# Two-bank PSUM tiles taken as two one-bank tiles in a fused RWKV-7 and gated feed-forward kernel

## The chip, the core and the metric

The kernel runs on one core of one Trainium2 chip. Five engines work side by side, each through its own queue in order: TensorE (PE in the profile; its weight loads are PEld), VectorE (DVE), ScalarE (ACT), GpSimd (POOL) and the DMA-issuing SyncE (SP). TensorE writes its results into PSUM, which this kernel uses as eight banks of 512 float32 per partition; VectorE and ScalarE read them from there. The metric is the device time of one execution in microseconds.

## The reference

Two blocks are computed one after the other, in float32 on the chip. The first is a recurrence over 768 time steps, for 4 batches of 8 heads with 40 features; the second is a feed-forward layer with `h * cos(h)` between two matrices.

```python
# attention block, per batch b and head h; state is 40 x 40
for t in range(S):
    y[:, :, t] = einsum('bhd,bhde->bhe', r_t, state)
    Sa = einsum('bhde,bhe->bhd', state, a_t)
    state = state * w_t[:, :, None, :] - einsum('bhd,bhe->bhde', Sa, b_t) \
          + einsum('bhd,bhe->bhde', v_t, k_t)
# feed-forward block on x = y as (3072 tokens, 320)
h = x @ w_in            # 320 x 2048
out = (h * cos(h)) @ w_out   # 2048 x 320
```

## The kernel before

The recurrence is done in 24 units, u = 0 to 23. A unit is 64 time steps of two batches with all their heads. Inside a unit the steps are dense matrices, and only the state passes from unit to unit of the same two batches. The work of a unit is cut into segments, each a short helper function that gives TensorE 4 to 64 small matmuls into a PSUM tile and then lets ScalarE or VectorE read that tile:

- `p1_w`, `p1_a`, `p1_b`, `p1_n` (for two units at a time): transposes of w, a and b (tiles wT, aps, bT), then the products of b and a within the unit (tile nps). ScalarE copies nps to `nt` (line 484), from which VectorE computes a triangular inverse in many small steps (lines 530 and 534); ScalarE later copies another part of nps (line 503).
- `p2_v`, `p2_k`, `p2_g`: transposes of v, r and k (tiles vT and kT), then the tile gram, which VectorE masks into `ag` (line 688) and `vvm` (line 692).
- `ch_t`, `ch_q`: the state is transposed (tile sT, ScalarE's copy `s` in line 708) and multiplied by r (tile qps); ScalarE copies the result into `qz` (line 721).
- `ch_ag`, `ch_xa`: the tile x0ps is filled in two parts and read by both engines, bank 0 by ScalarE (line 752) and bank 1 by VectorE (line 753).
- `ch_s`: the tile sps, the inverse times x0. ScalarE copies the state columns of both banks into `sm` (line 770, two instructions), VectorE masks the rest of both banks into `sm` (line 775, two instructions).
- `ch_z`: the tile dps. Its first half needs only kn and vvm, its second half `sm`. VectorE reads it in lines 801 and 812.

Beside this run the pieces of the feed-forward block: `first_a` and `first_b` fill two one-bank tiles ph in the pool `ps_h`. ScalarE rounds them (line 899), VectorE subtracts (line 903), ScalarE takes absolute value and sine (lines 906 and 907), VectorE multiplies into `gT` (line 910). `second` multiplies `gT` with w_out into the tile po of the pool `ps_o`, which ScalarE scales into `ot` (line 931).

All tiles of the recurrence's segments come from the pool `ps_a` through `at(name)`: a tile of two banks, and two such tiles, so four banks in all. Segments that need one bank (kT, sT, below, beside, xps) take a two-bank tile through `one(None, name)` and leave its second bank unused. A tile is given out again when all readers of its predecessor are done. A framework sets the semaphores, tile by tile: an instruction that touches a PSUM tile waits for the last one on another engine that touched the same tile, also where both only read and where their banks differ.

The order on every engine is written out by hand: `PLAN`, a list of some 1,900 words, each a segment (`xa9`, `s9`), a piece of the feed-forward block (`M`), one of the six later steps of a piece (`r`), a step of the inverse (`i`), a step of decoding the feed-forward weights (`c`) or a load (`Lk9`). `^` adds one dummy matmul on the identity ahead of the next tile (`busy`). The engines follow this order exactly; no scheduler moves anything. Loading of a weight piece (`seg_f`, SP's queue) is started from within `w_item` when a leading piece is done.

Of the kernel before, what the change touches and what calls it, by code (L numbers as in the profile page):

```python
# [20 lines left out]
def kernel(  # L21
# [38 lines left out]
    ps_a = ctx.enter_context(tc.tile_pool(name="ps_a", bufs=2, space=bass.MemoryType.PSUM))  # L60
# [311 lines left out]
    def p1_w(u):  # L372
        ps = at("wT")
        for i in range(2):
            turned(ps[:, i], nat["w", u + i])
        for i in range(2):
            if u < 4:
                nc.scalar.copy(G["w1"][:, i, :, 0:1], b4(ps[:, i])[:, :, 0:1])
                nc.vector.memset(ps[:, i, ::C], 0.0)
            wb = ring.tile([P, 4 * P + 1], F32, tag="wb", name="wb")  # L380
            if u < 4:
                nc.vector.tensor_tensor_scan(
                    wb[:, 1:], ps[:, i], flat(G["w1"][:, i]), 0.0, ALU.mult, ALU.add
                )
            else:
                nc.scalar.copy(wb[:, 1:], ps[:, i])
# [23 lines left out]
    def p1_a(u):  # L410
        if u >= 4:
            ps = at("aps")
            for i in range(2):
                turned(ps[:, i], nat["a", u + i])
            for i in range(2):
                a_W(u + i, ps[:, i])
# [13 lines left out]
    def p1_b(u):  # L430
        ps = at("bT")
        for i in range(2):
            turned(ps[:, i], bn_b[(u + i) % 7])
        for i in range(2):
            bT = sb3.tile([P, 4, P], F32, tag="opT", name="bT")
            nc.scalar.copy(bT.rearrange("p j t -> p (j t)"), ps[:, i])
            G["bT", u + i] = bT

    def p1_n(u):
        if u == 2:  # L440
            ps = [one(ps_h, "nps") for _ in range(2)]
        else:
            pair = at("nps")
            ps = [pair[:, e] for e in range(2)]
# [35 lines left out]
        else:  # L480

            for n in range(4):
                o = 8 * Q * (n % 2)
                nc.scalar.copy(
                    G["nt"][quad[n], :, u % 4 : u % 4 + 2],
                    pair[quad[n], :, o : o + 8 * Q].rearrange("p e (c j t) -> p t c e j", c=2, j=HH),
                )
# [171 lines left out]
    def p2_v(u):  # L659
        ps = at("vT")  # L660
        turned(ps[:, 0], nat["v", u])
        turned(ps[:, 1], nat["r", u])
        G["vT", u] = sb3.tile([P, 4, P], F32, tag="opT", name="vT")
        G["rT", u] = sb2.tile([P, 4, P], F32, tag="rT", name="rT")
        nc.scalar.copy(G["vT", u].rearrange("p j t -> p (j t)"), ps[:, 0])
        nc.scalar.activation(
            G["rT", u].rearrange("p j t -> p (j t)"), ps[:, 1], ACTF.Copy, scale=0.5 / math.pi
        )

    def p2_k(u):  # L670
        ps = at("kT")
        turned(ps[:, 0], kn_b[u % 2])
        G["kT", u] = sb3.tile([P, 4, P], F32, tag="opT", name="kT")
        nc.scalar.copy(G["kT", u].rearrange("p j t -> p (j t)"), ps[:, 0])

    def p2_g(u):
        kT, vT, aT, rT = G["kT", u], G["vT", u], G["aT", u], G["rT", u]
        ps = at("gram")
        for x, y, o in ((kT, aT, 0), (vT, rT, HH)):
            for j in range(4):  # L680
                for bb in range(NB):
                    for e in range(2):
                        mm(
                            ps[blk[bb], e, (o + j) * C : (o + j + 1) * C], x[half[e], j, blk[bb]],
# [3 lines left out]
        nc.vector.tensor_tensor(  # L688
            ag.rearrange("p (e j) t -> p e (j t)", e=2), ps[:, :, : HH * C],
            su.rearrange("p j t -> p (j t)").unsqueeze(1).to_broadcast([P, 2, HH * C]), ALU.mult,  # L690
        )
        nc.vector.tensor_tensor(
            pick(vvm[u % 2], 0, (HH * NW + D, 2), (NW, HH), (1, C)),
            ps[:, :, HH * C :].rearrange("p e (j t) -> p e j t", t=C),
            su.unsqueeze(1).to_broadcast([P, 2, HH, C]), ALU.mult,
        )
# [3 lines left out]
    def ch_t(u):  # L700
        ps = at("sT")
        z = qz[u % 2]
        G["s", u] = sb1.tile([P, 2 * NB, P], F32, tag="s", name="s")
        for i in range(2 * NB):
            nc.tensor.transpose(  # L705
                ps[:, 0, i * P : (i + 1) * P], z[:, i // 2, i % 2, C : C + P], ident
            )
        nc.scalar.copy(G["s", u].rearrange("p i e -> p (i e)"), ps[:, 0])

    def ch_q(u):  # L710
        ps = at("qps")
        z = qz[u % 2]
        for i in range(2 * NB):
            for e in range(2):
                for f in range(2):
                    mm(
                        ps[half[e], f, i * C : (i + 1) * C], G["s", u][half[f], i, half[e]],
                        G["rT", u][half[f], 2 * (i % 2) + e, blk[i // 2]], i == 0,
                    )
        for rows in half:  # L720
            nc.scalar.copy(  # L721
                pick(z[rows], 0, (NZ - C, 2), (NZ, 2 * NB), (1, C)),
# [554 lines left out]
```

## Time and profile before

| what | value |
|---|---|
| runs | 783.51, 782.81 and 779.36 us, median 782.81 us |
| profiled execution, its own time | 778.82 us |
| span of the profiled execution, first to last instruction | 776.9 us |
| TensorE busy | 752.7 us |
| VectorE busy | 504.9 us |
| ScalarE busy | 416.5 us |
| GpSimd busy | 184.0 us |
| mean granted TensorE clock | 0.994 |

A row of instruction groups reads: line, engine, operation, what is written and from what, shape, count, then busy time in us and the mean of one in ns, then the idle time of the engine just before these instructions and what ended it. A row of the waits reads: the waiting engine with tile and line, the releaser, then total us, times, longest us. A row of the timeline reads: start and duration in us, engine, line, operation, tiles, count, and in brackets the idle time before it with its releaser; neighbouring instructions of a kind are merged, so that the duration is that of the group. The ends of matmuls are modelled, so what counts for TensorE is when its next group starts.

### The profile page before, as it was taken

The page shows a single profiled execution, that of the slowest core. Times are in us where ns is not written, and L with a number is a line of the kernel's source. Part 1 is how long each engine was busy: PE and PEld are TensorE (multiplying, and loading weights), DVE is VectorE, ACT ScalarE, POOL GpSimd, SP SyncE. Part 2 cuts the span into 40 slices and gives each one's busy share as a digit, 9 for nine tenths or more (in the row PEclk, how much of TensorE's full clock was granted, in tenths as well). Part 3 has the DMA queues.
Part 4 walks back from the last instruction along what each step waited for, and adds up shares of the span by engine and source line. Part 5 has one row for each costly group of instructions (what it writes and reads, how often), then busy time and mean ns, then how long its engine had stood idle before and what let it go on. Part 6 is the DMA issues. An engine that isn't in the chain of part 4 may idle for free.

```text
span 776.9 us, 27804 instructions
## 1 busy us (share of the span) xinstructions
PE 752.7 (97%) x12118; PEld 593.5 (76%) x12118; DVE 504.9 (65%) x965; ACT 416.5 (54%) x762; POOL 184.0 (24%) x320
## 2 busy tenths in 40 slices
PE   8999999899999999999999999999999999999995
PEld 6877877677777877777878778787877787777773
DVE  6796889899769965578835677844476743334221
ACT  1354677655484566546475655465644464544432
POOL 5224635411331242120222202340101121201000
PEclk9999999999999999999999999999999999999998
DMA  9553675362334424423411421423022110200100
GB/s 141 113 128 76 151 183 141 94 140 42 59 103 79 88 61 77 112 72 61 83 34 38 96 62 21 87 54 71 3 46 55 34 23 19 56 10 16 33 17 18
DMA packets 180913, 54.36 MB, mean 70 GB/s; under 512 B 156344, under 2 KB 176440, under 8 KB 180792
## 3 DMA queue, kind: packets, MB, share of 16 engines
q1 hardware_dynamic: 173368, 51.43, 30.2%
q10 hardware_dynamic: 7424, 1.15, 1.0%
q8 instruction: 96, 1.57, 0.8%
q14 instruction: 25, 0.20, 0.1%
HBM read 41.68 MB, written 10.81 MB: 68 GB/s over the span
## 4 chain that ended last, share of the span: by engine, by line
PE 78%; DVE 10%; ACT 5%; issue 2%; DMA 2%; SPq 1%; POOL 1%; ACTq 0%; DVEq 0%; POOLq 0%
PE ph L75 24%; PE po L75 23%; PE dps L75 5%; PE x0ps L75 4%; PE beside L75 3%; PE gram L75 3%; PE sps L75 3%; DVE inv L534 2%; PE vT L364 2%; DVE inv_tmp L530 2%; PE nps L75 1%; PE below L75 1%; DMA words<-in_moe_w_in_dram 1%; PE bT L364 1%; PE qps L75 1%
## 5 line engine op out<-in xcount | busy, mean ns | idle before, releaser
L75 PE MATMUL po<-w_out_sb,gT 128*128 128x320 f32 x768 | 220.5, 438 | 0.0
L75 PEld LDWEIGHTS po<-w_out_sb,gT 128*128 128x128 f32 x768 | 141.3, 190 | 56.5 <-issue 2.4
L75 PE MATMUL ph<-xT,w_in_sb 128*128 128x256 f32 x768 | 183.2, 386 | 0.7 <-DVE gT L910 0.7
L75 PEld LDWEIGHTS ph<-xT,w_in_sb 128*128 128x128 f32 x768 | 140.6, 190 | 30.1 <-issue 9.4
L899 ACT ACTIVATE turns<-ph,rnd 128x512 f32<-128x512 f32 x96 | 62.9, 685 | 130.8 <-PE ph L75 129.7
L903 DVE SCALAR_TENSOR_TENSOR turns<-turns,ph 128x512 f32<-128x512 f32 x96 | 63.3, 679 | 79.7 <-ACT turns L899 79.6
L910 DVE TENSOR_TENSOR gT<-ph,turns 128x512 f32<-128x512 f32 x96 | 65.0, 684 | 33.4 <-ACT turns L907 33.1
L802 POOL TENSOR_TENSOR qz<-qz,wc 128x160 f32<-128x160 f32 x44 | 21.0, 480 | 221.2 <-DVE qz L801 220.3
L907 ACT ACTIVATE turns<-turns,half_pi 128x512 f32<-128x512 f32 x96 | 69.3, 722 | 3.1
L906 ACT ACTIVATE turns<-turns 128x512 f32<-128x512 f32 x96 | 60.2, 627 | 14.4 <-DVE turns L903 13.8
L534 DVE TENSOR_TENSOR inv<-inv,inv_tmp 128x31 f32<-128x31 f32 (+15 forms) x155 | 59.5, 384 | 5.3
L530 DVE TENSOR_TENSOR inv_tmp<-u,inv 128x31 f32<-128x31 f32 (+15 forms) x155 | 56.9, 367 | 3.1
L75 PE MATMUL ph<-xT,w_in_tail 64*64 64x256 f32 (+1 forms) x696 | 51.8, 383 | 0.0
L399 DVE RECIPROCAL rw<-nat_w 128x320 f32<-128x320 f32 x20 | 42.8, 2142 | 0.3 <-POOL kn L653 0.3
L817 POOL TENSOR_TENSOR yt<-yt,wb 128x512 f32<-128x512 f32 x24 | 31.2, 1302 | 42.5 <-DVE yt L812 42.4
L753 DVE COPY x<-x0ps 128x416 f32<-128x416 f32 x24 | 14.2, 591 | 38.6 <-ACT x L752 38.4
L721 ACT COPY qz<-qps 40x512 f32<-40x512 f32 x44 | 25.4, 577 | 22.4 <-PE qps L75 22.0
L75 PEld LDWEIGHTS ph<-xT,w_in_tail 64*64 64x64 f32 (+1 forms) x696 | 26.8, 138 | 13.6 <-issue 8.3
L400 POOL TENSOR_TENSOR bn<-nat_b,rw 128x320 f32<-128x320 f32 x22 | 19.3, 878 | 73.3 <-DVE rw L399 71.5
L775 DVE TENSOR_TENSOR sm<-sps,su 128x256 f32<-128x256 f32 x48 | 18.0, 417 | 25.1 <-ACT sm L770 21.4
L688 DVE TENSOR_TENSOR ag<-gram,su 128x512 f32<-128x512 f32 x24 | 16.5, 686 | 21.4 <-PE gram L75 21.3
L653 POOL TENSOR_TENSOR kn<-nat_k,rw 128x320 f32<-128x320 f32 x24 | 22.0, 915 | 31.7 <-PE sT L705 11.2
(181 smaller groups left out, 1178.0 us busy)
## 6 DMA issues: line engine op xcount, KB each, us to landing
rp<-in_r_dram SPq DMA_DIRECT2D x96, 40.0 KB
out_dram<-ot SPq DMA_DIRECT2D x24, 160.0 KB
vp<-in_v_dram SPq DMA_DIRECT2D x92, 40.0 KB
xd<-yt SPq DMA_DIRECT2D x44, 80.0 KB
nat_a<-in_a_dram SPq DMA_DIRECT2D x43, 80.0 KB
nat_k<-in_k_dram SPq DMA_DIRECT2D x42, 80.0 KB
nat_b<-in_b_dram SPq DMA_DIRECT2D x41, 80.0 KB
ws<-in_w_dram SPq DMA_DIRECT2D x5, 640.0 KB
```

Of the source, the lines that this page charges most:

```text
L75: nc.tensor.matmul(o, lhsT=lhsT, rhs=rhs, start=start, stop=stop, skip_group_check=True)
L364: nc.tensor.transpose(ps[:, i * P : (i + 1) * P], x[:, 2 * i : 2 * i + 2].rearrange("p e d -> p (e d)"), ident)
L399: nc.vector.reciprocal(rw, wn)
L530: nc.vector.tensor_tensor(tmp, u[:, j : j + 1, :j].to_broadcast([P, Q - j, j]), x[:, j:, j : j + 1].to_broadcast([P, Q - j, j]), ALU.mult,)
L534: nc.vector.tensor_tensor(x[:, j:, :j], x[:, j:, :j], tmp, ALU.subtract)
L721: nc.scalar.copy(pick(z[rows], 0, (NZ - C, 2), (NZ, 2 * NB), (1, C)), ps[rows, :, : 2 * NB * C].rearrange("p f (i t) -> p f i t", t=C),)
L817: nc.gpsimd.tensor_tensor(yt.rearrange("p j b t -> p (j b) t"), yt.rearrange("p j b t -> p (j b) t"), wx, ALU.mult)
L899: nc.scalar.activation(n, u, ACTF.Identity, bias=rnd, scale=1.0)
L903: nc.vector.scalar_tensor_tensor(ns[e], ns[e], -ROUND, us[e], ALU.add, ALU.subtract)
L906: nc.scalar.activation(n, n, ACTF.Abs)
L907: nc.scalar.activation(n, n, ACTF.Sin, bias=half_pi, scale=-2.0 * math.pi)
L910: nc.vector.tensor_tensor(gT[:, 2 * e : 2 * e + 2].rearrange("p f t -> p (f t)"), us[e], ns[e], ALU.mult)
```

## The change

`ps_a` gives four tiles of one bank each instead of two tiles of two banks. `at(name)` returns a list of two such tiles, and `one(None, name)` takes a single one, so that kT, sT, below, beside and xps occupy one bank. Every `ps[:, i]` becomes `ps[i]`. Readers that took both banks in one instruction are cut by bank:

- gram: two VectorE instructions of 512 elements per partition become four of 256 (`ag` for bank 0 and 1, then `vvm` for bank 0 and 1).
- qps: two ScalarE copies, each of 40 partitions and both banks, become two copies of all 128 partitions and one bank. For this TensorE computes 64 instead of 40 output partitions per matmul, with as many matmuls as before.
- nps, for units from 4 on: four ScalarE copies (one for each 32 partitions, both banks) become six, three for each bank: first all 128 partitions, then 32 partitions twice, which replace what the first wrote there.
- sps: the order becomes ScalarE bank 0, VectorE bank 1, ScalarE bank 1, VectorE bank 0. In each bank the second reader waits for the first.

The loads of weight pieces stand in `PLAN` as words of their own (`f7` and so on) at the places where they were started before. In the built program the order on GpSimd's and SyncE's queues is the same as before; on TensorE, ScalarE and VectorE it differs only in the instructions named here.

```diff
-    ps_a = ctx.enter_context(tc.tile_pool(name="ps_a", bufs=2, space=bass.MemoryType.PSUM))
+    ps_a = ctx.enter_context(tc.tile_pool(name="ps_a", bufs=4, space=bass.MemoryType.PSUM))
...
-    def at(name):
-        ps = ps_a.tile([P, 2, 512], F32, tag="at", name=name)
-        busy(ps[:, 0])
-        return ps
+    def at(name, n=2):
+        tiles = []
+        for _ in range(n):
+            tiles.append(ps_a.tile([P, 512], F32, tag="at", name=name))
+            busy(tiles[-1])
+        return tiles
 
     def one(pool, name):
         if pool is None:
-            return at(name)[:, 0]
+            return at(name, 1)[0]
...
     def p1_n(u):
-            for n in range(4):
-                o = 8 * Q * (n % 2)
-                nc.scalar.copy(
-                    G["nt"][quad[n], :, u % 4 : u % 4 + 2],
-                    pair[quad[n], :, o : o + 8 * Q].rearrange("p e (c j t) -> p t c e j", c=2, j=HH),
-                )
+            for e in range(2):
+                for n in (0, 1, 3):
+                    rows, o = quad[n] if n else every, 8 * Q if n else 0
+                    nc.scalar.copy(
+                        G["nt"][rows, :, u % 4 : u % 4 + 2, e, :],
+                        ps[e][rows, o : o + 8 * Q].rearrange("p (c j t) -> p t c j", c=2, j=HH),
+                    )
...
     def p2_g(u):
-        nc.vector.tensor_tensor(
-            ag.rearrange("p (e j) t -> p e (j t)", e=2), ps[:, :, : HH * C],
-            su.rearrange("p j t -> p (j t)").unsqueeze(1).to_broadcast([P, 2, HH * C]), ALU.mult,
-        )
+        for e in range(2):
+            nc.vector.tensor_tensor(
+                ag[:, HH * e : HH * (e + 1)], b4(ps[e])[:, :HH], su, ALU.mult
+            )
...
     def ch_q(u):
-                        ps[half[e], f, i * C : (i + 1) * C], G["s", u][half[f], i, half[e]],
+                        ps[f][full[e], i * C : (i + 1) * C], G["s", u][half[f], i, full[e]],
...
-        for rows in half:
+        for f in range(2):
             nc.scalar.copy(
-                pick(z[rows], 0, (NZ - C, 2), (NZ, 2 * NB), (1, C)),
-                ps[rows, :, : 2 * NB * C].rearrange("p f (i t) -> p f i t", t=C),
+                pick(z, f * (NZ - C), (NZ, 2 * NB), (1, C)), b4(ps[f][:, : 2 * NB * C]),
             )
...
     def ch_xa(u):
-        nc.scalar.copy(x0[0], ps[:, 0, : 4 * NW])
-        nc.vector.tensor_copy(x0[1], ps[:, 1, : 4 * NW])
+        nc.scalar.copy(x0[0], ps[0][:, : 4 * NW])
+        nc.vector.tensor_copy(x0[1], ps[1][:, : 4 * NW])
...
     def ch_s(u):
-        for e in range(2):
+        def state(e):
             nc.scalar.copy(
                 pick(sm[e], C, (2 * NW - C, 2), (NW, 2), (1, D)),
-                pick(ps[:, e], C, (2 * NW - C, 2), (NW, 2), (1, D)),
+                pick(ps[e], C, (2 * NW - C, 2), (NW, 2), (1, D)),
             )
-        for e in range(2):
+
+        def masked(e):
             nc.vector.tensor_tensor(
                 pick(sm[e], 0, (2 * NW + D, 2), (NW, 2), (1, C)),
-                pick(ps[:, e], 0, (2 * NW + D, 2), (NW, 2), (1, C)),
+                pick(ps[e], 0, (2 * NW + D, 2), (NW, 2), (1, C)),
                 su.rearrange("p (f m) t -> p f m t", f=2), ALU.mult,
             )
+
+        state(0)
+        masked(1)
+        state(1)
+        masked(0)
```

More of the change, by code (lines that the diff above doesn't have):

```diff
@@ L442, in p1_n @@
         else:
-            pair = at("nps")
-            ps = [pair[:, e] for e in range(2)]
+            ps = at("nps")
         for i in range(2):
@@ L660, in p2_v @@
         ps = at("vT")
-        turned(ps[:, 0], nat["v", u])
-        turned(ps[:, 1], nat["r", u])
+        turned(ps[0], nat["v", u])
+        turned(ps[1], nat["r", u])
         G["vT", u] = sb3.tile([P, 4, P], F32, tag="opT", name="vT")
         G["rT", u] = sb2.tile([P, 4, P], F32, tag="rT", name="rT")
-        nc.scalar.copy(G["vT", u].rearrange("p j t -> p (j t)"), ps[:, 0])
+        nc.scalar.copy(G["vT", u].rearrange("p j t -> p (j t)"), ps[0])
         nc.scalar.activation(
-            G["rT", u].rearrange("p j t -> p (j t)"), ps[:, 1], ACTF.Copy, scale=0.5 / math.pi
+            G["rT", u].rearrange("p j t -> p (j t)"), ps[1], ACTF.Copy, scale=0.5 / math.pi
         )
     def p2_k(u):
-        ps = at("kT")
-        turned(ps[:, 0], kn_b[u % 2])
+        ps = one(None, "kT")
+        turned(ps, kn_b[u % 2])
         G["kT", u] = sb3.tile([P, 4, P], F32, tag="opT", name="kT")
-        nc.scalar.copy(G["kT", u].rearrange("p j t -> p (j t)"), ps[:, 0])
+        nc.scalar.copy(G["kT", u].rearrange("p j t -> p (j t)"), ps)
     def p2_g(u):
@@ L687, in p2_g @@
         ag = sb1.tile([P, H, C], F32, tag="ag", name="ag")
-        nc.vector.tensor_tensor(
-            ag.rearrange("p (e j) t -> p e (j t)", e=2), ps[:, :, : HH * C],
-            su.rearrange("p j t -> p (j t)").unsqueeze(1).to_broadcast([P, 2, HH * C]), ALU.mult,
-        )
[L692 to L696, printed above, removed]
+        for e in range(2):
+            nc.vector.tensor_tensor(
+                ag[:, HH * e : HH * (e + 1)], b4(ps[e])[:, :HH], su, ALU.mult
+            )
+        for e in range(2):
+            nc.vector.tensor_tensor(
+                pick(vvm[u % 2], e * (HH * NW + D), (NW, HH), (1, C)),
+                b4(ps[e])[:, HH:], su, ALU.mult,
+            )
         G["ag", u] = ag
     def ch_t(u):
-        ps = at("sT")
+        ps = one(None, "sT")
         z = qz[u % 2]
@@ L789, in ch_z @@
                         mm(
-                            ps[(half if s else full)[e], bb, j * NW : (j + 1) * NW],
+                            ps[bb][(half if s else full)[e], j * NW : (j + 1) * NW],
                             n[blk[bb], 2 * j + e, : D if s else DP],
@@ L830, in straight @@
             G["xT", u // 2] = sb2.tile([P, 3, 2 * P], F32, tag="xT", name="xT")
-        ps = at("xps")[:, 0]
+        ps = one(None, "xps")
         for i, j in ((0, 0), (0, 1), (1, 1), (1, 2), (1, 3)):
@@ L1126, in w_item @@
                 w_count[0] += 1
-                if m in follower:
-                    seg_f(follower[m])
+                done.add(name)
+        leader = {n: m for m, n in follower.items()}
         def seg_f(m):
+            if m in leader:
+                needs(f"p{leader[m]}")
             if m == 13:
```

112 lines of the change are left out of this document (56 added, 56 removed).

## The prediction

> **What bounds the kernel now.** I began with the page's list of engines and its chain of work that ended last.
>
> ```profile
> PE 752.7 (97%) x12118; PEld 593.5 (76%) x12118; DVE 504.9 (65%) x965; ACT 416.5 (54%) x762; POOL 184.0 (24%) x320
> ...
> PE 78%; DVE 10%; ACT 5%; issue 2%; DMA 2%; SPq 1%; POOL 1%; ACTq 0%; DVEq 0%; POOLq 0%
> ```
>
> TensorE is the bound, and the change takes no matmul from it. What can be won is TensorE's idle time alone. The busy time by stretches shows where that lies; the columns are the stretch, its length, then busy us and instructions of each engine.
>
> ```profile
> 0.00:150.00 150.00, 139.42 (x2593) 112.46 (x2594) 122.71 (x221) 76.76 (x146) 63.99 (x115) 0.99 0.58 129
> 150.00:460.00 310.00, 305.05 (x5156) 241.65 (x5155) 227.26 (x453) 181.11 (x336) 75.22 (x133) 1.00 0.36 78
> 460.00:704.00 244.00, 243.72 (x4028) 191.94 (x4026) 134.73 (x261) 130.73 (x235) 42.25 (x70) 1.00 0.18 38
> 704.00:777.00 73.00, 64.53 (x356) 47.47 (x344) 20.18 (x33) 27.85 (x46) 2.55 (x2) 0.96 0.07 22
> ```
>
> Idle are 10.6, 4.9, 0.3 and 8.5 us. The last is the tail after the last matmuls, which the change doesn't touch. So at most some 16 us are to be had, all before 460 us; after that point TensorE can only lose. The table of waits says which of these 16 us have to do with two readers in one tile, or with a tile that wasn't free yet.
>
> ```profile
> DVE x L753 <- ACT x L752: 38.4, 19, 7.8
> DVE sm L775 <- ACT sm L770: 21.4, 8, 6.3
> PE dps L75 <- DVE ws L176: 2.2, 1, 2.2
> PE sps L75 <- DVE x L753: 1.1, 3, 0.7
> PE dps L75 <- DVE sm L775: 0.9, 2, 0.7
> PE ph L75 <- DVE gT L910: 0.7, 2, 0.5
> PE sT L705 <- ACT rt L647: 0.4, 1, 0.4
> PE gram L75 <- DVE x L753: 0.2, 1, 0.2
> ```
>
> VectorE stands 59.8 us behind ScalarE in line for a bank that ScalarE doesn't read. That looks like much, but TensorE's own waits in these rows are only 5.5 us: most of VectorE's waiting is covered by feed-forward matmuls.
>
> **The change, part by part.** *x0ps.* In the built program VectorE's copy now waits for TensorE and no longer for ScalarE. Around 140 us, where TensorE waits longest, the rows are:
>
> ```profile
> 139.32 0.51 ACT L752 COPY x<-x0ps 128x416 f32<-128x416 f32 x1
> ...
> 137.12 0.69 DVE L281 SCALAR_TENSOR_TENSOR w_in_sb<-w_in_sb,w_out_sb 128x512 f32<-128x512 f32 x1
> 139.86 0.59 DVE L753 COPY x<-x0ps 128x416 f32<-128x416 f32 x1 [2.05 <-ACT x L752]
> 144.11 0.76 DVE L775 TENSOR_TENSOR sm<-sps,su 128x256 f32<-128x256 f32 x2
> ...
> 143.62 0.45 ACT L770 COPY sm<-sps 128x160 f32<-128x160 f32 x2
> ...
> 140.50 0.94 PE L75 MATMUL sps<-x,rt 64*64 64x104 f32 x32 [0.65 <-DVE x L753]
> 145.01 0.94 PE L75 MATMUL dps<-vvm,kn 64*64 64x104 f32 x32 [2.15 <-DVE ws L176]
> ```
>
> VectorE is free at 137.81 and copies then; ScalarE still ends at 139.83, and sps can start there instead of at 140.50. With the two other waits of that row all 1.1 us go. The dps tile at 145.01 reuses the tile of sps and waits for its last reader, VectorE's sm, which ends at 144.87. VectorE's work between the two comes up to 2 us earlier, but ScalarE also has to come, so I take 0.3 us beyond the 0.65, between 0 (ScalarE holds it) and 1.5.
>
> *The turn of a feed-forward piece.* At 452 us the same wait delays something else:
>
> ```profile
> 451.62 0.49 ACT L752 COPY x<-x0ps 128x416 f32<-128x416 f32 x1
> ...
> 452.14 0.59 DVE L753 COPY x<-x0ps 128x416 f32<-128x416 f32 x1 [1.48 <-ACT x L752]
> 455.72 0.68 DVE L910 TENSOR_TENSOR gT<-ph,turns 128x512 f32<-128x512 f32 x1
> ...
> 456.46 1.99 PE L75 MATMUL ph<-xT,w_in_sb 128*128 128x256 f32 x8 [0.48 <-DVE gT L910]
> 458.69 1.99 PE L75 MATMUL ph<-xT,w_in_sb 128*128 128x256 f32 x8 [0.23 <-DVE gT L910]
> ```
>
> The two products in line 910 stand in VectorE's queue behind x. Without the 1.48 us of idle time they come that much earlier, more than TensorE waits, so 0.7 us go.
>
> *sps.* Before, two ScalarE and two VectorE instructions ran one after the other (0.45 and 0.76 us in the rows at 143.62 and 144.11, 1.2 us together); now each engine takes a bank, then they swap. With both free that is two times the slower one, 2 x 0.415 us by the group below, some 0.4 us less. The row of dps waiting for sm (0.9 us, twice) loses 0.3 each time, 0.6 us; bounds 0 and 0.9.
>
> *Tiles that come free.* sT and gram wait 0.6 us, for a tile whose second bank nobody used and for one whose VectorE reader was late. With four banks given out one by one, a segment finds its bank free sooner and never later, since a predecessor is always at least as far back. I take 0.5 us, between 0 and 0.6.
>
> *Split instructions.*
>
> ```profile
> L721 ACT COPY qz<-qps 40x512 f32<-40x512 f32 x44 | 25.4, 577 | 22.4 <-PE qps L75 22.0
> L484 ACT COPY nt<-nps 32x512 f32<-32x512 f32 x40 | 23.0, 575 | 9.3 <-PE nps L75 8.9
> L688 DVE TENSOR_TENSOR ag<-gram,su 128x512 f32<-128x512 f32 x24 | 16.5, 686 | 21.4 <-PE gram L75 21.3
> L775 DVE TENSOR_TENSOR sm<-sps,su 128x256 f32<-128x256 f32 x48 | 18.0, 417 | 25.1 <-ACT sm L770 21.4
> ...
> L476 ACT COPY nt<-nps 128x256 f32<-128x256 f32 x4 | 1.3, 375 | 3.0 <-PE nps L75 3.0
> ```
>
> qps: 44 copies from 577 ns to the 375 ns of a 128x256 copy, 8.9 us less on ScalarE. nps: 40 x 575 ns become 60 of about 375 ns, 22.5 instead of 23.0 us. gram: 48 instructions of about 686 ns become 96 of about 417 ns, 7.1 us more on VectorE and 0.3 us more between gram and x0ps. None of it enters TensorE's time where feed-forward pieces lie between; all of it is busy time off the bound, so I take 0, with bounds of -1 us (qz sooner) and +2 us (7.1 us over 24 units, a quarter of them seen).
>
> *Where a wait is added.* ScalarE's second copy of sps now waits for VectorE's mask of that bank. Where VectorE comes late, ScalarE stands, and everything in its queue with it. In 8 of 24 units VectorE was the early one (the second row of the waits); in 16 it came later. The costliest place that I found:
>
> ```profile
> 434.08 0.49 ACT L770 COPY sm<-sps 128x160 f32<-128x160 f32 x2 [1.11 <-PE sps L75]
> 434.46 0.64 ACT L906 ACTIVATE turns<-turns 128x512 f32<-128x512 f32 x1
> 437.28 1.07 ACT L436 COPY bT<-bT 128x512 f32<-128x512 f32 x2 [0.15 <-PE bT L364]
> ...
> 435.17 0.75 DVE L775 TENSOR_TENSOR sm<-sps,su 128x256 f32<-128x256 f32 x2
> ...
> 438.65 1.11 PE L75 MATMUL nps<-aT,bT 40*64 40x64 f32 x64
> ```
>
> ScalarE's second copy starts when VectorE's first mask ends, at 435.17 + 0.42 = 435.59, and ends near 435.9. Line 906 then starts 1.4 us late, the two turns behind it run without a gap to bT, bT ends at 439.6 or later instead of 438.35, and TensorE's nps, which started 0.3 us after bT, stands for 1.2 us. In the other units that I followed, ScalarE waits for TensorE soon after anyway, or feed-forward matmuls lie between its delay and TensorE. I take +1.2 us; bounds 0 and the price of the second rival.
>
> *TensorE's own instructions.* What qps costs with 64 instead of 40 output partitions, and what a satisfied wait inside a segment costs, show in two more rows:
>
> ```profile
> 433.12 0.90 PE L75 MATMUL sps<-x,rt 64*64 64x104 f32 x32
> ...
> 437.94 0.89 PE L75 MATMUL dps<-sm,bn 64*40 64x104 f32 x32
> ```
>
> sps has 64 output partitions, the second half of dps has 40, at the same count: 0.01 us, 0.2 us over 22 units. In the built program TensorE's matmuls with a wait go from 513 to 665, those that signal from 430 to 605, and its instructions that only wait from 307 to 292. sps right behind x at 140.50 took 0.94 us, and 0.90 at 433.12 with x long done: a wait inside a segment costs 0.04 us at most. I take 0, as waits ahead of segments fall away at the same time; upper bound 187 more tiles x 0.04 = 7.5 us. The Trainium skill, "TensorE: Matmul & The Clock Gate", section "The cost: per-tile semaphore tail", speaks against the change here: signals of matmuls on several array tiles are taken one after the other, at about 26 ns each. By that page 175 more signals would be an estimated 4.6 us if all lay on the path, and the sum below would be +2.6 instead of -2.0 us; no row of the profile before shows such a tail by itself.
>
> **The sum.** -1.1 (sps) - 0.3 (dps) - 0.7 (ph) - 0.6 (sm) - 0.5 (tiles) + 1.2 (ScalarE held up) = -2.0 us. The profiled execution took 778.82 us, so 776.8 us under its conditions. It is 4.0 us below the median of the three runs, 782.81 us; taken from that median, the forecast is 780.8 us, 0.3% faster.
>
> **The rivals.** *Stalls only move.* Where TensorE comes earlier it waits for the next thing, a DMA or VectorE, which is busy 82% in the first 150 us; ScalarE's lateness at 143.62 speaks for it, the unbroken TensorE after 460 us against it. All gains but none of the losses vanish into it: 782.8 us or 1 us more.
>
> *ScalarE waits for VectorE at sm.* The place is line 770; it decides once the added stalls pass the 3.2 us of gains. At 339 us ScalarE would be held longest:
>
> ```profile
> 337.67 2.15 DVE L399 RECIPROCAL rw<-nat_w 128x320 f32<-128x320 f32 x1
> ...
> 337.95 0.47 ACT L770 COPY sm<-sps 128x160 f32<-128x160 f32 x2
> ```
>
> VectorE is in a reciprocal until 339.82, so ScalarE stands until about 340.2 instead of leaving at 338.42. If the 16 units cost about 1 us each (between nothing and this 1.8) and half reach TensorE, that is +8, net +4.8: 787.6 us. For it speaks that ph and nps often start within a few tenths of their releaser, against it that ScalarE is idle 46% of the time.
>
> *TensorE pays for the split.* The upper bound of 7.5 us in full: 782.8 - 2.0 + 7.5 = 788.3 us. What the Trainium skill says of signals would stand here.
>
> *VectorE's freedom is worth more.* 59.8 us of its waits go, and lines 530, 534 and 910, which stand behind them, come earlier everywhere. Then of the 15.5 us of idle time before 460 us all but the start-up goes (some 6 us, first loads and first scans), and the delays of ScalarE are hidden: -9 us, 773.8 us. Against it: the waits by name that could go are 5.5 us.
>
> That the change doesn't do what it says is excluded for x0ps by the built waits; for sps one handshake per bank stays.
>
> **How the numbers follow.** The forecast has 0.40 (its own range 778 to 782.5), stalls that only move 0.13, ScalarE held up 0.20, TensorE paying 0.07, more from VectorE 0.20. A measurement of this kernel, with runs 0.5% apart, can't tell less than 0.5%, 3.9 us. Faster by more than that: the last rival and some of the forecast's gains above my values, 0.36. Within 0.5%: the rest of the forecast and stalls that move, 0.38. Slower: 0.26. The range goes from the last rival, with a run that is 1 to 2 us quick, to the price of the slower ones: 772 to 788.5 us.
>
> **What would show it.** The rows of VectorE's x and sm waiting for ScalarE should be gone or small, and ScalarE's sm should wait for VectorE's sm in about 16 units. TensorE's waits on x, gT at 456 us and sT should be gone; near 438 us nps should wait for bT. Line 721 should read about 375 ns, line 688's successor about 417 ns. TensorE's idle time before 460 us tells between the forecast (13 us), the last rival (6) and ScalarE held up (20 or more, also after 460 us). If the segments themselves take longer from start to start, TensorE pays. The prediction is wrong if TensorE's idle time grows, or if its waits shrink by far more than 3 us.

## The result, and the profile after

The changed kernel takes 773.99 us (median of 773.06, 776.38, 773.99, 774.05 and 773.92), against 782.81 us before, which is now the median of five. The ratio of the means is 0.9897, with a 95% interval of 0.9870 to 0.9925: 1.0% faster, where 0.3% was forecast. The profiled execution took 773.06 us, its span is 771.1 us, 5.8 us less than the span before. The medians differ by 8.8 us; so 3 us of the difference are not in the two traces (the section on the reasons comes back to that).

The page's list of engines:

```profile
PE 750.9 (97%) x12118; PEld 594.0 (77%) x12118; DVE 505.4 (66%) x1013; ACT 404.1 (52%) x782; POOL 185.0 (24%) x320
```

TensorE still sets the time, with the same work. VectorE has 48 instructions more and only 0.5 us more work, ScalarE 20 more and 12.4 us less. The busy time by stretches (stretch, length, then busy us and instructions of PE, PEld, DVE, ACT and POOL, then the granted clock, which is the share of its full speed that TensorE's clock was given, the DMA share and GB/s):

```profile
0.00:150.00 150.00, 140.67 (x2606) 114.00 (x2608) 125.00 (x232) 76.57 (x152) 65.36 (x116) 0.99 0.58 131
150.00:460.00 310.00, 307.58 (x5267) 244.52 (x5264) 229.82 (x483) 174.75 (x348) 74.86 (x133) 1.00 0.36 77
460.00:704.00 244.00, 244.00 (x3928) 192.33 (x3927) 133.87 (x273) 127.98 (x242) 43.52 (x71) 1.00 0.18 39
```

Idle on TensorE before 460 us are 9.3 + 2.4 = 11.75 us, 3.8 us less than before; after 460 us nothing, as nothing was lost there. The table of waits (who waits for whom: total us, times, longest):

```profile
DVE x L754 <- PE x0ps L75: 28.7, 12, 7.8
ACT sm L771 <- DVE sm L777: 17.4, 22, 2.2
DVE sm L777 <- ACT sm L771: 3.2, 2, 2.9
PE gram L75 <- ACT kT L676: 3.2, 1, 3.2
PE dps L75 <- ACT sm L771: 1.2, 2, 1.0
PE ph L75 <- DVE gT L917: 0.9, 2, 0.6
PE sps L75 <- ACT x L753: 0.3, 1, 0.3
```

VectorE's copy of x waits for TensorE alone, and its 59.8 us behind ScalarE have shrunk to 3.2 us. In their place ScalarE waits 17.4 us for VectorE at sps, in 22 units. One wait of TensorE has grown: for kT, from 1.2 to 3.2 us.

The place that the prediction looked at most closely, 139 to 146 us, in the timeline (start, us, engine, line, operation, and in brackets the idle time before it):

```profile
137.06 2.32 PE L75 MATMUL po<-w_out_sb,gT 128*128 128x320 f32 x8
139.70 0.94 PE L75 MATMUL sps<-x,rt 64*64 64x104 f32 x32 [0.32 <-ACT x L753]
142.65 0.94 PE L75 MATMUL dps<-vvm,kn 64*64 64x104 f32 x32 [0.99 <-ACT sm L771]
144.13 1.11 PE L75 MATMUL nps<-aT,bT 40*64 40x64 f32 x64
...
137.70 0.58 DVE L754 COPY x<-x0ps 128x416 f32<-128x416 f32 x1
...
141.87 0.74 DVE L777 TENSOR_TENSOR sm<-sps,su 128x256 f32<-128x256 f32 x2
```

sps no longer waits for VectorE. What changed more is further on: VectorE reaches sm at 141.87 instead of 144.11 us, and TensorE's wait at dps falls from 2.15 to 0.99 us.

### The profile page after: what moved, and what is told of

It reads as the page before. It is cut to its first block, busy times and chain, and to the rows that moved or that the text cites. A ratio compares the mean times of both kernels' runs of the same rounds, so it can differ in the third digit from the quotient of the medians.

```text
span 771.1 us, 27824 instructions
## 1 busy us (share of the span) xinstructions
PE 750.9 (97%) x12118; PEld 594.0 (77%) x12118; DVE 505.4 (66%) x1013; ACT 404.1 (52%) x782; POOL 185.0 (24%) x320
## 4 chain that ended last, share of the span: by engine, by line
PE 71%; DVE 10%; ACT 2%; issue 2%; DMA 2%; POOL 1%; SPq 0%; DVEq 0%; POOLq 0%; ACTq 0%
PE ph L75 24%; PE po L75 24%; PE x0ps L75 4%; PE dps L75 4%; PE beside L75 2%; PE gram L75 2%; PE sps L75 2%; DVE inv L536 2%; PE vT L366 2%; DVE inv_tmp L532 2%; DMA words<-in_moe_w_out_dram 2%; PE nps L75 1%; PE qps L75 1%; PE kT L366 1%; PE sT L707 1%
## 5 line engine op out<-in xcount | busy, mean ns | idle before, releaser
L917 DVE TENSOR_TENSOR gT<-ph,turns 128x512 f32<-128x512 f32 x96 | 65.1, 683 | 35.8 <-ACT turns L914 35.7
L691 DVE TENSOR_TENSOR ag<-gram,su 128x256 f32<-128x256 f32 x48 | 18.0, 416 | 25.0 <-PE gram L75 25.0
L771 ACT COPY sm<-sps 128x160 f32<-128x160 f32 x48 | 13.8, 292 | 34.1 <-DVE sm L777 17.4
```

What stands on the lines that cost most here:

```text
L917: nc.vector.tensor_tensor(gT[:, 2 * e : 2 * e + 2].rearrange("p f t -> p (f t)"), us[e], ns[e], ALU.mult)
```

## The experiments

All are built on the changed kernel unless said otherwise. The kernel before was run beside each group; its median there was 783.76 us for the first four, 782.12 us for the next four, 784.79 us for the next three and 782.71 us for the last. A ratio is to the kernel before of its own group, so ratios are what compares runs of different groups.

| run | median us | ratio (95% interval) | span us of the profile |
|---|---|---|---|
| x_in_line | 780.22 | 0.9952 (0.9935 to 0.9969) | 777.7 |
| scalar_first | 771.77 | 0.9838 (0.9819 to 0.9857) | 771.3 |
| two_banks | 773.94 | 0.9871 (0.9855 to 0.9888) | 771.9 |
| sign_later | 773.88 | 0.9872 (0.9851 to 0.9893) | 772.6 |
| load_on_sync | 767.79 | 0.9815 (0.9791 to 0.9838) | 765.9 |
| dummies_moved | 769.73 | 0.9827 (0.9803 to 0.9850) | 765.3 |
| masks_behind_both | 774.01 | 0.9888 (0.9865 to 0.9912) | 772.0 |
| before_again | 778.74 (one) | none | 776.9 |
| both_in_line | 779.74 | 0.9941 (0.9921 to 0.9960) | 779.1 |
| before_load_on_sync | 778.80 | 0.9926 (0.9903 to 0.9950) | 781.3 |
| after_load_on_sync | 768.99 | 0.9793 (0.9771 to 0.9815) | 766.9 |
| x_in_line_once | 776.26 | 0.9910 (0.9879 to 0.9941) | 776.5 |

**x_in_line: the x readers one behind the other again.**

```diff
-        nc.scalar.copy(x0[0], ps[0][:, : 4 * NW])
-        nc.vector.tensor_copy(x0[1], ps[1][:, : 4 * NW])
+        first = nc.scalar.copy(x0[0], ps[0][:, : 4 * NW])
+        behind(nc.vector.tensor_copy(x0[1], ps[1][:, : 4 * NW]), first)
```

`behind` adds a dependency, and so a semaphore wait, of the later instruction on the sooner one.

> The changed kernel, but VectorE's copy of x waits for ScalarE's again, through an added dependency; all else stays split. The forecast's terms: what the x split won is the three waits of sps (1.1 us), 0.3 us at dps, 0.7 us at ph, so the span grows from 771.1 by about 2.1 to 773.2 us, and TensorE's rows of sps waiting for x (1.1 us, 3) and ph for gT near 456 us come back. The last rival, VectorE's freedom is worth more everywhere: 38.4 of the 59.8 us of VectorE's waits return, and with them two thirds of the 5.9 us, 3.9 us: span 775.0 us, and TensorE's idle time before 460 us goes from 11.75 back towards 15.5 us. If the gain has little to do with x: within 0.5 us of 771.1.

Measured: 780.22 us, 6.2 us more than the changed kernel (and than two_banks and sign_later in its own group, 773.94 and 773.88 us), and a span longer by 6.6 us. That is three times the forecast's terms and more than the last rival's two thirds. Within its group it is still 0.3 to 0.65% faster than the kernel before, so by the ratios the order at x is about half of the change's 1.0%. The timeline shows the largest piece of it:

```profile
139.71 0.59 DVE L761 COPY x<-x0ps 128x416 f32<-128x416 f32 x1 [1.91 <-ACT x L760]
...
143.88 0.74 DVE L784 TENSOR_TENSOR sm<-sps,su 128x256 f32<-128x256 f32 x2
...
140.35 0.94 PE L75 MATMUL sps<-x,rt 64*64 64x104 f32 x30 [0.23 <-DVE x L761]
144.67 1.25 PE L75 MATMUL dps<-vvm,kn 64*64 64x104 f32 x32 [2.36 <-ACT sm L778]
145.67 1.63 PE L75 MATMUL dps<-sm,bn 64*40 64x104 f32 x32
147.06 1.81 PE L75 MATMUL nps<-aT,bT 40*64 40x64 f32 x64
```

At sps TensorE loses some 0.6 us. VectorE's 1.91 us are carried through everything behind x in its queue (aT, the decoding of the weights, gT): sm starts at 143.88 instead of 141.87, and dps waits 2.36 us. Behind that wait the same matmuls take 1.63 and 1.81 us instead of 0.89 and 1.11: the clock has fallen.

**x_in_line_once: the same in one unit only**, `if u == 3: behind(last, first)`.

> The changed kernel, with VectorE's copy of x behind ScalarE's in one of the 24 units alone, the fourth, whose sps starts near 139.7 us. With all units in line, TensorE lost 3.5 of its 6.6 us between 140.6 and 145.2 us, in that unit: 0.5 us at sps, 1.4 us at dps (VectorE reaches sm 2 us later), and 1.6 us in dps and nps at half clock behind that wait. If the gain of the x split is one place, its wait and its clock, this run loses 3.5 us: span 774.6, median near 777.5 us. If the clock stays at 1.0 behind the wait, 1.9 us: 773 us span. If what counted was VectorE's freedom in all units together, the loss at this one is hidden later and the run stays within 1 us of 771.1 us span and 774.0 us median.

Measured: 776.26 us, 2.3 us more than the changed kernel; the interval of the ratio overlaps that of the changed kernel, so the times alone don't show this difference, and it is read from the trace:

```profile
139.25 2.32 PE L75 MATMUL po<-w_out_sb,gT 128*128 128x320 f32 x8
...
146.63 1.66 PE L75 MATMUL dps<-vvm,kn 64*64 64x104 f32 x32 [2.36 <-ACT sm L780]
...
149.46 1.17 PE L75 MATMUL nps<-aT,bT 40*64 40x64 f32 x64
```

From the start of po to the start of nps this unit takes 10.21 us (149.46 - 139.25) against 7.07 us in the changed kernel (144.13 - 137.06), and the 3.1 us last to the end. The other 2.2 us by which this span is longer are there at 139.25 us already (po started at 137.06 in the changed kernel), and so don't come from the edit: near 40 us the wait for kT is 3.9 instead of 3.2 us, and the clock stands at half for 6.8 instead of 3.4 us. So, by the traces, this one unit holds about half of what x is worth; the other half is spread over the other units (in x_in_line 1.3 us of it at the turn of a feed-forward piece near 456 us).

**scalar_first and masks_behind_both: the order at sps.** In the first, ScalarE copies both banks and VectorE follows a bank behind; in the second VectorE waits until both are copied, the order of the kernel before.

```diff
-        state(0)
-        masked(1)
-        state(1)
-        masked(0)
+        state(0)
+        second = state(1)
+        behind(masked(0), second)    # only in masks_behind_both
+        masked(1)
```

> The changed kernel, but at sps ScalarE copies both banks in a row and VectorE masks them behind it, bank 0 first; ScalarE never waits for VectorE there. If the swap costs what the forecast says (ScalarE held up, 1.2 us at nps near 438 us), the 17.4 us of ScalarE's waits for VectorE's sm go, nps and po near 439 us are about 1.0 us sooner, and the span is about 770 us. What the overlap of the two engines at sps was put at, 0.3 us at each of two waits of dps, comes back as +0.6 us in the same run: net -0.4 us, 770.7 us. If the hold-up is hidden everywhere, 771.1 us or some tenths more. If the swap was what won the unforeseen part, 2 us or more slower: 773 us.

> ScalarE first at sps, and VectorE's two masks wait until ScalarE has copied both banks, as in the kernel before; the banks stay split. The forecast put the overlap of the two engines at sps at 0.3 us for each of two waits of dps: 0.6 us slower than 771.8, 772.4 us. If the freedom at sps is worth more, as that at x was (6 us back, ratio 0.9952), 2 to 3 us slower: 774 us. If x alone makes the change: 771.8 us.

Measured: 771.77 us for ScalarE first, 774.01 us with both masks behind, 773.99 us for the swap of the changed kernel. The swap is worth no more than the old order (ratios 0.9897 and 0.9888). Letting VectorE follow bank by bank is 2.2 us better than both by the medians, more than I expected (0.4 us against the swap). Against the old order the intervals are apart; against the swap in the same group, two_banks, they just touch. The spans don't show the gain (771.3 and 771.1 us): the profiled execution is the longest of the five, 773.29 us, and near 40 us its clock stands at half for 6.8 instead of 3.4 us. The price of the swap is seen near 434 us, in the changed kernel and then with ScalarE first:

```profile
427.79 0.90 PE L75 MATMUL sps<-x,rt 64*64 64x104 f32 x32
...
430.40 0.29 ACT L771 COPY sm<-sps 128x160 f32<-128x160 f32 x1 [1.37 <-DVE sm L777]
...
433.78 0.33 PE L75 MATMUL nps<-aT,bT 40*64 40x64 f32 x2 [0.28 <-ACT bT L438]
...
435.36 2.42 PE L75 MATMUL po<-w_out_sb,gT 128*128 128x320 f32 x8
```

```profile
429.00 0.90 PE L75 MATMUL sps<-x,rt 64*64 64x104 f32 x32
...
435.57 2.42 PE L75 MATMUL po<-w_out_sb,gT 128*128 128x320 f32 x8
```

From sps to po: 7.57 us with the swap, 6.57 us without, as in the kernel before. ScalarE stands 1.37 us for VectorE, its two turns and bT come late, nps waits, po follows: 1.0 us, where the prediction worked out 1.2. Where the rest of the 2.2 us lies is not shown.

**two_banks: one-bank users take two banks again** (`return at(name, 2)[0]`, and the same for kT and sT).

> The changed kernel, but a user of one bank takes two again, and leaves the second empty. The forecast put the earlier free tiles at 0.5 us (sT near 106 us, gram near 308 us): span 771.6 us, with sT waiting at 106 us again. If the banks given out one by one are where the unforeseen 3 us come from: 774 us or more. If no segment needed them: 771.1 us.

Measured: 773.94 us, no difference from 773.99. The wait of sT, 0.4 us in the kernel before, doesn't come back in this trace, so it went for another reason than the free bank. The 0.5 us of earlier free tiles are not seen, but so little is below what these medians can tell.

**both_in_line: x_in_line and masks_behind_both together.**

> The split banks, but every reader in the order of the kernel before: VectorE's copy of x waits for ScalarE's, and both masks at sps wait until ScalarE has copied both banks. What is left of the change is the split itself: more and shorter instructions on VectorE and ScalarE, 175 more signals of TensorE, and banks given out one by one. The forecast put the split at nothing and the tiles at 0.5 us: ratio to the kernel before 0.999 to 1.000, about 782 to 783 us. If TensorE pays for the split (the third rival, 7.5 us at most; VectorE's 7 us more of work come on top), the ratio is 1.003 to 1.010. If the split instructions themselves win (qz and nt sooner), 0.996 or less.

Measured: 779.74 us, ratio 0.9941. With the readers of x and sps in the old order the split kernel does not pay for its shorter instructions and its signals, and by the times it gains 0.4 to 0.8%. Its profile does not show that gain: its span, 779.1 us, is 2.1 us longer than the span before, with the clock at half twice, near 41 and near 147 us. One thing of the split stays that the expectation doesn't list: the reader of a first bank no longer waits for the matmuls of the second. Near 438 us ScalarE starts to copy bT before TensorE's transposes into bT end:

```profile
438.01 1.04 PE L366 MATMUL bT<-ident,bn 128*128 128x128 f32 x8
...
438.83 1.05 ACT L438 COPY bT<-bT 128x512 f32<-128x512 f32 x2
```

At 9 of the 12 tiles bT of this run the copy starts 0.64 to 0.82 us after the first transpose; in the kernel before it is 1.07 us at the least. Whether the 0.4 to 0.8% come from this is not shown.

**sign_later, load_on_sync, dummies_moved: the new wait at 38 us.** The changed kernel's TensorE and ScalarE there:

```profile
38.68 0.69 PE L75 MATMUL gram<-aT,kT 40*64 40x64 f32 x32 [3.21 <-ACT kT L676]
...
40.56 4.22 PE L75 MATMUL kT<-ident 128*128 128x256 f32 x12
...
30.98 6.33 ACTq L144 DMA_DIRECT2D nat_k<-in_k_dram  x2
37.36 0.66 ACT L264 ACTIVATE sign<-words 128x512 bf16<-128x512 int32 x1 [6.66 <-DMA w_out_sb<-in_moe_w_in_dram]
38.04 0.59 ACT L676 COPY kT<-kT 128x512 f32<-128x512 f32 x1
```

Either the sign's DMA or the issue of the load of k could hold ScalarE. In the list of steps `PLAN`, the three runs change one thing each (parts of lines; the last two on top of scalar_first):

```diff
-  Lk1a i i wj1 c f1 i f2 i i i ^ ^ ^ ^ ^ ^ k0 i i
+  Lk1a i i wj1 f1 i f2 i i i ^ ^ ^ ^ ^ ^ k0 c i i
...
-  lo0 i i Lk1a i i wj1
+  lo0 i i Lk1 i i wj1
...
-  Lv1a ^ g0 i i Lr1 f3 K1 ^ ^ ^ ^ ^ ^ k1
+  Lv1a ^ ^ ^ ^ ^ ^ ^ g0 i i Lr1 f3 K1 k1
```

> The changed kernel, with one step moved in the written order: the sign of the first weight words (on ScalarE behind a DMA that lands near 37.3 us) and VectorE's mask of them come after ScalarE's copy of kT instead of ahead of it. In the changed kernel TensorE was 4.4 us ahead of the kernel before at 39 us and lost 4.0 us there, waiting 3.2 us for kT. If that wait is ScalarE's queue held by the DMA, it goes, and TensorE is 3 to 4 us ahead of the changed kernel at 75 us. Whether it lasts: if VectorE's chain of block inverses (busy 82% in the first 150 us) sets the rest of that stretch, TensorE waits the same 3 us later, between 90 and 145 us, and the span stays within 1 us of 771.1; if TensorE sets it, the span is 767 to 768 us. If kT came late for another reason, the wait at 38 us stays.

> ScalarE first at sps, as in the run before (771.77 us, ratio 0.9838), and one load moved: the second unit's k, which ScalarE's queue issues near 31 us, goes to the sync engine's queue. Theory: ScalarE stands from 31 to 37.3 us in the issue of that load's second half, and kT, vT, rT behind it come late, so TensorE waits 3.2 us at 38.7 us and then runs at half clock for 3.5 us (the 12 dummy matmuls took 4.2 to 4.6 us instead of 2.86). Without it the copy of kT starts near 32 us, the wait is gone, and TensorE is 4 to 5 us ahead at 48 us. If that stretch sets the start of the rest, the run is at 767 to 769 us; if VectorE's chain of inverses (its last step near 44 us, then two transposes of 2 us each) takes over, 1 to 2 us remain: 770 us. Rival (kT is late for the sign of the weight words, or the start-up is cushioned anyway): no change, 771.8 us, ratio 0.984.

> ScalarE first at sps, and six of the dummy matmuls that stand ahead of the second unit's kT are put ahead of the first unit's gram, into TensorE's wait of 3.2 us. Their number is unchanged. Theory: the clock falls to 0.5 because TensorE stands for about 3 us; with dummies in the wait the clock stays at 1.0 between 38 and 44 us, and the second kT starts right behind gram, some 4 us sooner (2.9 us of dummies and 1.4 us of slow clock). End 1 to 3 us sooner than 771.8 if nothing else holds that stretch; 771.8 if VectorE's inverse does. Rival (the clock falls for another reason): the profile still shows 0.5 near 40 us.

Measured: moving the sign changes nothing (773.88 us; TensorE waits 2.37 us for kT and then 0.85 us for rT, against 3.21 and 0.29 us). Moving the load does: 767.79 us, 4.0 us less than scalar_first by the medians, and ScalarE copies kT at once:

```profile
31.59 0.58 ACT L676 COPY kT<-kT 128x512 f32<-128x512 f32 x1 [0.26 <-PE kT L366]
...
35.33 0.69 PE L75 MATMUL gram<-aT,kT 40*64 40x64 f32 x32
36.42 2.86 PE L75 MATMUL kT<-ident 128*128 128x256 f32 x12
```

So it is the issue of the load that holds ScalarE. In the built program the load's second half waits for a semaphore that it shares with the load of a 512 KB piece of weights on another queue, issued at 30.9 us; the issue itself starts only at 36.7 us. The spans of scalar_first and load_on_sync are 5.4 us apart, 3.4 us of which are the clock, which stays up in load_on_sync; the intervals of their ratios overlap, so the size of the gain is not sharp. Six dummies in the wait instead of behind it give 769.73 us, by its interval not told apart from scalar_first, but the wait for kT is down to 0.23 us, and the clock stays at 1.00 between 40 and 44 us where it had fallen (first the changed kernel, then dummies_moved; stretch, length, PE busy, granted clock, DMA share, GB/s):

```profile
40.00:42.00 2.00, 2.00 (x31) 0.50 1.00 289
42.00:44.00 2.00, 2.00 (x8) 0.66 0.39 63
```

```profile
40.00:42.00 2.00, 2.00 (x35) 1.00 0.93 279
42.00:44.00 2.00, 2.00 (x22) 1.00 0.67 189
```

**before_load_on_sync and after_load_on_sync**: the same load moved in the kernel before and in the changed kernel.

> The kernel before with one load moved: the second unit's k goes to the sync engine's queue. In the kernel before, TensorE waits 1.2 us at 39.3 us for kT, which ScalarE copies late for the same reason (the issue of that load ends at 37.9 us). So 1.2 us of wait, and the copy's lateness for VectorE, which waits for gram: 1.5 to 3 us less, ratio 0.996 to 0.998. If the change's early 4.4 us were lost only there, this run with the next one shows a larger difference than the two kernels without the move (9 us).

> The changed kernel with the same load moved (the swapped order at sps stays). Against the changed kernel (ratio 0.9897): TensorE's wait of 3.2 us and the 1.4 us of slow clock near 40 us go, as in the run with ScalarE first, 4 to 5 us: ratio 0.984, 769 to 770 us. Against the run before this one: if the start-up swallowed part of the change, the difference grows from 9 us to 11 us or more; if not, it stays at 9 us.

Measured: 778.80 and 768.99 us. The difference is 9.8 us, where it is 8.8 us without the move; by the intervals of the two ratios it can be anything from some 8 to 13 us, so these runs don't tell whether the start-up hides a part of the change. The kernel before gains 6.0 us by the move within its group (3.9 to 7.6 us by the interval), more than the 1.2 us of its wait at 39 us can explain. The rest goes with the clock: five of its six executions have a mean granted clock of 0.994 to 0.998, the kernel before in the same group 0.987 to 0.994. The sixth, 783.10 us at a clock of 0.989, is the one that was profiled, and it shows the clock falling, behind the wait at dps:

```profile
145.77 0.94 PE L75 MATMUL dps<-vvm,kn 64*64 64x104 f32 x32 [2.16 <-DVE ws L176]
146.50 1.30 PE L75 MATMUL dps<-sm,bn 64*40 64x104 f32 x32
147.50 2.00 PE L75 MATMUL nps<-aT,bT 40*64 40x64 f32 x64
...
155.62 0.70 PE L75 MATMUL ph<-xT,w_in_tail 64*128 64x256 f32 x4
```

From dps to the tail products it takes 9.85 us; the kernel before took 6.60 us in its profile (145.01 to 151.61) behind the same wait of 2.15 us. The granted clock makes the difference (this run, then the kernel before; columns as above):

```profile
148.00:150.00 2.00, 2.00 (x59) 0.50 0.42 65
150.00:152.00 2.00, 2.00 (x6) 0.50 0.39 78
```

```profile
148.00:150.00 2.00, 2.00 (x11) 1.00 0.20 28
150.00:152.00 2.00, 2.00 (x12) 1.00 0.52 123
```

**before_again: a second profile of the kernel before.**

> The kernel before, once more, for a second profile. Its first profiled execution took 778.82 us, 4.0 us less than its median. Theory: executions differ by whether TensorE's clock falls after a wait of 2 to 3 us near 39 us and near 145 us (the first profile shows 1.00 at both, after waits of 1.2 and 2.2 us). A profile nearer to the median of 783 us would then show the granted clock at 0.5 for some 3 us behind one of these waits. If it shows 1.00 everywhere and is 4 us longer, something else differs between executions; if it is as short as the first, this run tells nothing.

Measured: 778.74 us and a span of 776.9 us, the same as the first profile, with the clock at 1.00 at 39 and 145 us. It tells nothing of the executions near the median.

## Why the prediction was right or wrong

- **The direction was right, and so was where to look**: before 460 us, TensorE's idle time alone. The size was not: -2.0 us in the sum, -5.8 us between the spans, -8.8 us between the medians. The measured time lies in the stated range (772 to 788.5 us) through the last rival, which had a chance of 0.20, and not through the forecast, whose own range began at 778 us.
- **x at sps, 1.1 us**: right in kind. At 140 us sps now waits 0.32 us for ScalarE, so 0.8 us of the 1.1 are gone.
- **"so I take 0.3 us beyond the 0.65"**, at dps: this is the step that failed. The wait fell by 1.2 us (2.15 to 0.99), and x_in_line and x_in_line_once put the place at 2.9 to 3.1 us from po to nps, with the clock. The prediction saw that VectorE's work comes up to 2 us earlier and bounded the term at 1.5 us; it took a value near the lower bound for fear of ScalarE, and it priced a wait by its length alone.
- **The other waits, put at nothing**: the same step, taken for all other places. The table of the kernel before has 2.7 us of waits of TensorE that no term names: for aT 1.5 us, as below, for s 0.6, for half 0.4, for rt 0.2 us. None of these rows is left in the changed kernel. Which part of the change took each is open: x_in_line has 0.5 us for aT again, both_in_line none.

```profile
PE sps L75 <- DVE aT L405: 0.6, 1, 0.6
PE beside L75 <- DVE aT L405: 0.6, 1, 0.6
...
PE bT L364 <- DVE aT L405: 0.3, 1, 0.3
```

- **ph at 456 us, 0.7 us**: right place. From the last transpose to the tail products it took 5.23 us before (455.38 to 460.61) and takes 3.99 us now: 1.2 us. Another wait of ph for gT, 0.6 us near 116 us, is new.
- **sm, 0.6 us**: the two waits of dps for sm, 0.9 us before, are down to one of 0.2 us (the other one in the table is the place above). Whether the overlap at sps did this is not shown: with the 1.2 us that ScalarE is held up, the prediction had the swap 0.6 us worse than the old order, and the times (773.99 and 774.01 us) can't tell that from nothing. What it didn't think of is a third order, ScalarE first and VectorE a bank behind, 2.2 us better by the medians.
- **Tiles free sooner, 0.5 us**: the run with two banks each shows none of it.
- **ScalarE held up, 1.2 us**: right in place, chain and size (1.0 us).
- **Split instructions, 0, and TensorE's own, 0**: not contradicted. The copies of qz read 371 ns and the masks of gram 416 ns (forecast 375 and 417), and both_in_line, which has all of them, is not slower than before. But the masks of gram (ag and vvm) cost VectorE 3.0 us more (32.8 to 35.8 us), not 7.1, since neighbouring instructions overlap, as those of line 775 did before (48 of 417 ns in 18.0 us). The estimated 4.6 us that the Trainium skill would give ("TensorE: Matmul & The Clock Gate", section "The cost: per-tile semaphore tail") do not appear; no run here shows that tail.

Matmul by matmul, the two traces show where the 5.8 us come from. Compared with the kernel before, TensorE is 1.3 us late at 52 us and even at 132 us; then it is 2.3 us ahead behind the dps above, 4.9 us ahead at 340 us (in small steps), 4.3 us at 440 us behind the held-up ScalarE, 5.6 us at 461 us behind ph, 5.9 us at the end.

Of the rivals, *VectorE's freedom is worth more* came nearest with 773.8 us, and x_in_line confirms its cause for 6 of the 9 us by the medians, for about half by the ratios. Its detail is not confirmed: idle time before 460 us is 11.75 us, not 6, and about half of x's worth is one unit. Part of the first rival, stalls that only move, is also seen: TensorE reaches gram's dummies 4.4 us sooner than before (34.87 against 39.30 us) and the second kT 0.9 us later (44.61 against 43.72 us), since the wait for kT and the slow clock lie between. Some 1.7 of these 4.4 us are themselves the clock: it stands at half from 20.4 to 23.8 us in the kernel before (0.60 and 0.55 in the rows from 20 to 24 us), and in the changed kernel only from 39.9 to 43.3 us. All that the change gains in the traces it gains after that.

The 3 us that are in the medians and not in the spans go with the clock. The record has 46 more executions of the kernel before, run beside the experiments, each with its mean granted clock: the 13 with 0.993 or more took 781.5 us on average, the 23 with 0.990 or less 784.5 us, and in each of the four groups the first are shorter, by 2 to 5 us. The two profiled executions had 0.994 and took 778.8 us; four of the five of the changed kernel had 0.995. Where the kernel before loses its clock no trace of it shows; in before_load_on_sync it is behind the wait at dps, which the change shortens. That this is the place in the kernel before too is likely, not shown.

What stays open is the other half: with the readers of x and sps in line again the split kernel is still 0.4 to 0.8% faster by the times. The clock alone doesn't make it: at 0.993 or more, six of its executions took 779.7 us on average and three of the kernel before in its group 783.5 us.

The fastest kernels here are load_on_sync and after_load_on_sync, 767.79 and 768.99 us: 1.6 to 2.3% less than the kernel before by their two intervals. Which order at sps is better beside that move can't be told from these two.

## What to carry to other kernels

With a framework that orders accesses tile by tile, two engines that read different banks are in line for nothing if the banks belong to one tile; look at what stands behind the waiting reader in its queue, and price the delay at the end of that queue, not at the reader's own consumer. When both engines need both banks, try one that goes first through all of them and the other a bank behind; a swap makes each wait for the other, and here it won nothing. A wait of TensorE, here even one of 1.8 us, costs more than itself if the clock falls behind it.

## What was not expected of the hardware

TensorE's granted clock fell to 0.5 after waits of some 2 us, and not each time. The 2.16 us at dps in before_load_on_sync were followed by 6.8 us at half clock, the 3.21 us at gram in the changed kernel by 3.4 us (0.50 and 0.66 in the two rows above), while the 2.15 us at dps in the kernel before were followed by none, in both its profiles. A shorter wait with a fall behind it is one of 1.83 us, in two_banks (a row of its timeline, then one of its stretches, columns as above):

```profile
120.04 0.70 PE L75 MATMUL dps<-ident 128*128 128x256 f32 x2 [1.83 <-ACT sm L771]
...
122.00:124.00 2.00, 2.00 (x40) 0.50 0.62 186
```

In all traces a fall between matmuls lasts either 3.4 or 6.8 us. At half clock that is an estimated 1.7 or 3.4 us on top of the wait; behind dps in before_load_on_sync it was 3.25 us (9.85 less 6.60). The Trainium skill, "TensorE: Matmul & The Clock Gate", section "Why this matters for your kernels", asks for no idle gaps over about 3 us between bursts of matmuls; here single gaps of 1.8 to 2.4 us were enough in several runs, and the measurement decides. In the kernel before, two waits of 1.11 and 0.65 us (ending at 18.14 and 19.89 us) stood ahead of the fall at 20.4 us.

Dummy matmuls kept the clock up where they filled the wait. In dummies_moved 14 records of them run into the free bank of gram from 34.53 us on, 0.23 us of wait for kT remain, and the clock stays at 1.00. In the changed kernel only two of these records ran there, at 34.87 us, 3.21 us of waiting followed, and the clock fell.
